# The first batch of an attention and mixing kernel run group by group, with joint folds and a second bank for the first products

## The chip, the cores and the metric

The kernel runs on one core of a Trainium2 chip. The metric is device time in microseconds (us), the median of several executions. One further execution was taken by the hardware profiler; its rows are times within that one execution, counted from the start of its span. Engines are named PE (TensorE, matrix products), DVE (VectorE), ACT (ScalarE), POOL (GpSimd) and SP (the engine that issues most loads and stores).

## The reference

The inputs are q, k, v of shape (8, 8, 576, 64) (batch, heads, positions, head size), 32 packed queries p for each head, and two weights of 512x2048 and 2048x512.

```python
def sm_attn(qq, kk, vv):
    s = scale * np.matmul(qq, kk.transpose(0, 1, 3, 2))
    s = s - np.max(s, axis=-1, keepdims=True)
    a = np.exp(s)
    a = a / (np.sum(a, axis=-1, keepdims=True) + 1e-09)
    return np.matmul(a, vv)
p_packed = sm_attn(p, k, v)
out = sm_attn(q, p_packed, p_packed)
# x = out with the heads side by side: (8, 576, 512)
X = np.fft.fft(x, axis=1)
X = np.fft.fft(X, axis=2)
u = x + np.real(X)
mu = np.mean(u, axis=-1, keepdims=True)
var = np.mean((u - mu) ** 2, axis=-1, keepdims=True)
un = (u - mu) / np.sqrt(var + 1e-06)
ch = np.maximum(un @ w_ch1, 0.0) @ w_ch2
return u + ch
```

## The kernel before

Each batch has a front (attention and the two Fourier transforms, which give rows of u) and then shares of nine tiles of 512 rows through the two weight products. The fronts of batches 1 to 7 run in between the products of the tile before; the front of batch 0 has nothing ahead of it. Products of 32-bit values are made from a high and a low part (`split`: ScalarE rounds to the high part, another engine takes the rest), three products for one.

**The front** works on two groups g of four heads. Its steps have one letter each, and a written list `ORDER` (one string for batch 0, one for the others) sets their order; as scheduling is manual for PE, DVE, ACT and POOL, each engine executes its instructions as this order issues them. In batch 0: K, V, Q, B, W load keys, values, queries, tables and weight blocks on SP; S makes the scores of the packed queries and their exponentials for both groups (`scores`, tiles s1 and s1t in the code, s and s1t in the profile), t turns them, p and c make the packed values (pp) and a block diagonal of them (bd, and its parts bdh, bdl), d and l turn and split those (ppT, pph, ppl); U makes the scores of the queries (s2T) for both groups, u turns them on VectorE (`turned_queries`), e subtracts the maximum and exponentiates (`less_one`), m subtracts the mean (`less_mean`), w and b scale and turn to a (`scaled`, `upright`). G makes products of the packed values with a Fourier basis (pg), T turns their phases (`values_turned`), z splits the result into gh and gl. f folds a by its symmetries into eo and f (`folded`), r makes the small rest of f (`folded_rest`, on GpSimd in batch 0), h splits f into fh and fl, x splits eo (xh, xl, oh, ol). P multiplies fh, fl with gh, gl for all six parts of the spectrum (`waves_of`, the waves py) and splits each into yh and yl behind the second group. H unpacks a weight block on ScalarE (`halves_of`), `joined` ends that on VectorE, and L issues the loads of four tables on GpSimd and one on SP.

After the waves, `value` multiplies the parts of eo with the block diagonal (px) and `spectrum` the splits with the tables (pz, copied to spec); from both VectorE makes pe, qe and then two blocks of 128 rows of u, twice. `Turned` subtracts the mean (un), turns a block on PE (untp) and splits it (uh, ul).

**The products.** `up(j)` multiplies uh, ul with weight block j of w1 into a bank ph, ScalarE and VectorE make hh and hl of it, and `down(j)` multiplies these with block j of w2 into four accumulators. The weight blocks' parts wr_h (ScalarE) and wr_l (GpSimd) come from a generator, `splits`. The first `up` runs in two halves of 256 rows in one bank.

**PSUM** has eight banks: four accumulators, one for ph, and a ring of three (tag `ps`). `bank` takes the next one of the ring or, while the accumulators are spare (in batch 0's front), one of these. A tile that is taken from the ring waits for the last reader of the tile three before it.

The order behind the front's list is in the code that calls it, with `next(gen0)` for each stretch of batch 0's generator up to its next yield:

```python
        next(gen0)
        for k in (0, 2):
            joined(k // 2, k % 2)
        next(splits)
        next(splits)
        ...
        centred(3)
        cur.parts(2)
        cur.parts(3)
        for k in (1, 3, 4, 5):
            joined(k // 2, k % 2)
```

## Time and profile before

| | us |
|---|---|
| Median of 3 executions | 989.1 (988.87 to 991.14) |
| Profiled execution, whole | 990.03 |
| Profiled execution, span of its instructions | 988.3 |
| PE busy | 952.2 (96% of the span) |
| VectorE busy | 555.2 (56%) |
| ScalarE busy | 474.4 (48%) |
| GpSimd busy | 469.1 (47%) |
| First product of up(0) | 54.49 |
| First product of up(1) | 64.63 |

A row of a timeline has the start in us, the length, the engine, the line of the kernel, the operation, the tile written and those read, partitions and columns, and a count if several were merged; in brackets stands how long the engine was idle before it and what ended that. The chain of waits is followed back from the last instruction to what released each. A PE row's length holds the time through the array, so that rows overlap; the distance from start to start is what a product costs in a stream. PE's rows of 32-bit operands come twice, as two passes.

### The profile page before, as it was taken

Reading aid. Unit: us, or ns where it says so; the run is one execution under the profiler, and the core shown is the slowest. Engines: PE = TensorE matmul, PEld = TensorE weight load, DVE = VectorE, ACT = ScalarE, POOL = GpSimd, SP = SyncE. Lnnn points to the kernel's source line nnn. Section 1 sums busy time; section 2 is a strip of 40 time slices with the busy share of each in tenths; the row PEclk is TensorE's granted clock in tenths of the full one; section 3 lists DMA queues with packets and bytes.
Section 4 is the critical chain, followed back from the end, with each engine's and each line's share of the span. In section 5 each row is a group of like instructions: output and inputs, shape, how many; then the busy total and the mean of one; then the engine's idle time right before and its main releaser. Section 6 shows DMA issues by size and latency. Waiting matters only on the chain.

```text
span 988.3 us, 15063 instructions
## 1 busy us (share of the span) xinstructions
PE 952.2 (96%) x5588; PEld 783.8 (79%) x5588; DVE 555.2 (56%) x1224; ACT 474.4 (48%) x956; POOL 469.1 (47%) x409
## 2 busy tenths in 40 slices
...
GB/s 363 114 75 203 161 180 65 127 26 1 20 136 63 1 2 141 49 1 22 100 118 0 9 60 162 9 1 55 136 49 1 22 65 1 1 31 55 1 1 43
DMA packets 28170, 65.94 MB, mean 67 GB/s; under 512 B 5494, under 2 KB 12992, under 8 KB 28096
## 3 DMA queue, kind: packets, MB, share of 16 engines
...
q8 instruction: 44, 0.72, 0.3%
q14 instruction: 30, 0.25, 0.1%
...
## 4 chain that ended last, share of the span: by engine, by line
PE 90%; DVE 4%; ACT 3%; DMA 1%; issue 1%; POOL 0%; SPq 0%; DVEq 0%; ACTq 0%; POOLq 0%
PE ph L780 38%; PE acc L795 38%; PE po L323 1%; PE py L236 1%; PE py L234 1%; PE py L235 1%; PE px L234 1%; PE px L236 1%; PE px L235 1%; PE e1tp L300 1%; PE s L266 1%; PE s2T L266 1%; PE pz L234 1%; PE pz L236 1%; PE pz L235 1%
## 5 line engine op out<-in xcount | busy, mean ns | idle before, releaser
L100 POOL TENSOR_TENSOR wr_l<-w1f,wr_h 128x512 fp32r<-128x512 f32 x144 | 194.6, 1352 | 280.1 <-ACT wr_h L99 237.9
L785 DVE SCALAR_TENSOR_TENSOR hl<-ph,hh 128x512 fp32r<-128x512 f32 x144 | 98.9, 687 | 335.6 <-ACT hh L784 335.2
L100 POOL TENSOR_TENSOR wr_l<-w2f,wr_h 128x512 fp32r<-128x512 f32 x144 | 192.3, 1336 | 173.1 <-ACT wr_h L99 166.3
L780 PE MATMUL ph<-uh,wr_h 128*128 128x512 f32 (+1 forms) x580 | 228.7, 395 | 3.8 <-DVE hl L785 2.3
L795 PE MATMUL acc<-wr_h,hh 128*128 128x512 f32 x576 | 226.2, 393 | 0.0
L780 PE MATMUL ph<-uh,wr_l 128*128 128x512 f32 (+1 forms) x580 | 225.4, 389 | 0.0
L795 PE MATMUL acc<-wr_h,hl 128*128 128x512 f32 x576 | 225.2, 391 | 0.0
L795 PE MATMUL acc<-wr_l,hh 128*128 128x512 f32 x576 | 225.2, 391 | 0.0
L780 PE MATMUL ph<-ul,wr_h 128*128 128x512 f32 (+1 forms) x580 | 220.8, 389 | 0.0
L784 ACT ACTIVATE hh<-ph 128x512 fp32r<-128x512 f32 x144 | 86.2, 599 | 206.4 <-PE ph L780 192.3
L780 PEld LDWEIGHTS ph<-uh,wr_h 128*128 128x128 f32 x580 | 108.9, 188 | 38.8 <-DVE mx L285 5.9
L780 PEld LDWEIGHTS ph<-uh,wr_l 128*128 128x128 f32 x580 | 108.9, 188 | 23.1
L795 PEld LDWEIGHTS acc<-wr_h,hl 128*128 128x128 f32 x576 | 108.2, 188 | 23.2
L780 PEld LDWEIGHTS ph<-ul,wr_h 128*128 128x128 f32 x580 | 109.0, 189 | 20.7
L795 PEld LDWEIGHTS acc<-wr_h,hh 128*128 128x128 f32 x576 | 108.2, 188 | 21.8
L795 PEld LDWEIGHTS acc<-wr_l,hh 128*128 128x128 f32 x576 | 108.2, 188 | 21.3
L99 ACT CAST wr_h<-w1f 128x512 fp32r<-128x512 f32 x144 | 88.9, 618 | 55.9 <-POOL wr_l L100 54.2
L99 ACT CAST wr_h<-w2f 128x512 fp32r<-128x512 f32 x144 | 88.3, 613 | 12.4 <-PE acc L795 8.1
L234 PE MATMUL py<-gh,fh 128*128 128x258 f32 (+2 forms) x96 | 29.1, 303 | 14.4 <-ACT fh L529 14.4
L213 ACT ACTIVATE junk<-ubuf,stat 128x512 f32<-128x512 f32 x36 | 25.6, 713 | 25.0 <-DVE stat L209 25.0
L100 POOL TENSOR_TENSOR gl<-turned,gh 128x516 fp32r<-128x516 f32 x16 | 24.6, 1535 | 26.3 <-ACT gh L99 26.3
L236 PE MATMUL py<-gh,fl 128*128 128x258 f32 (+2 forms) x96 | 29.0, 302 | 2.6 <-DVE fl L531 2.6
...
## 6 DMA issues: line engine op xcount, KB each, us to landing
...
w1f<-w SPq DMA_DIRECT2D x3, 512.0 KB, 10.4
```

What stands on the lines that cost most here:

```text
L99: nc.scalar.copy(hi, src)
L100: (lo_eng or nc.vector).tensor_tensor(lo, src, hi.bitcast(F32), ALU.subtract)
L213: nc.scalar.activation(junk, u, AF.Square, bias=st[:, 1:2], scale=1.0, accum_out=st[:, 2:3])
L234: nc.tensor.matmul(o, lh, rh, start=first, stop=False)
L235: nc.tensor.matmul(o, lh, rl, start=False, stop=False)
L236: nc.tensor.matmul(o, ll, rh, start=False, stop=last)
L266: nc.tensor.matmul(res[g][c][at, :w.stop - w.start], lhs(g, h), rhs(g, h, w), start=True, stop=True, tile_position=(r, h * NPK))
L300: nc.tensor.transpose(tp[g][:, c * P:(c + 1) * P], e1s[g][:, c * P:(c + 1) * P], ident)
L780: nc.tensor.matmul(ph[:, t], l[:, c * P:(c + 1) * P], r[:, c, t], start=(n == 0), stop=(n == 11))
L784: nc.scalar.activation(hh[:, :T], ph[:, :T], AF.Relu)
L785: nc.vector.scalar_tensor_tensor(hl[:, :T], ph[:, :T], 0.0, hh[:, :T].bitcast(F32), ALU.max, ALU.subtract)
L795: nc.tensor.matmul(acc[i], l[:, w], r, start=(j == 0 and k == 0), stop=(j == NJ - 1 and k == 2))
```

## The change

- **By group.** In batch 0 the scores S and the queries U are issued for one group at a time (s0, s1, q0, q1), and the turn of the queries (v0, v1) stands in each group's own part of the list. The list's other steps move too: ScalarE's weight blocks H, the loads L (now behind gl and s of group 1 on GpSimd), and the splits z of gh and gl.
- **Joint folds.** In `folded` two instructions make what four made: both halves of a pair in one access pattern with a step between them (`pair`). `folded_rest` does the same with its small parts. This holds for all batches.
- **Parts of f.** In batch 0 fh and fl are made in two pieces, columns 0 to 421 and 421 to 776.
- **Waves.** Their order changes, the last of them takes the bank ph, and the first two px are made between the waves of group 0 and those of group 1 (X). The join and the split of the first weight block come behind the fourth wave.
- **First products.** The first `up` takes two banks, ph and one of the ring, for its two halves; it makes the products with the high parts of both halves first, then those with the low parts. Blocks 2 and 3 of u are turned in banks of the ring, between the two halves. The low parts of u, five joins and the split of two weight blocks come behind that.

VectorE, from the last rows of u to the first hl. Before, two of the ul (low parts of u) stood ahead of these rows (L640), and four joins (L174) behind the other two:

```order
L100 TENSOR_TENSOR ul<-untp,uh 128x4x4x32 [waits Activation_49] x2
L640 SCALAR_TENSOR_TENSOR ubuf,stat<-qe,pe 128x512 [waits DVE_49]
L209 TENSOR_SCALAR stat<-stat 128x1 [waits DVE_49]
L640 SCALAR_TENSOR_TENSOR ubuf,stat<-qe,pe 128x512
L209 TENSOR_SCALAR stat<-stat 128x1 [waits DVE_49]
L100 TENSOR_TENSOR ul<-untp,uh 128x4x4x32 [waits Activation_49] x2
L174 SCALAR_TENSOR_TENSOR w2f<-w2f 128x512 [waits DMAHW2_49]
L174 SCALAR_TENSOR_TENSOR w2f<-w2f 128x512 [waits DMAHW4_49]
L174 SCALAR_TENSOR_TENSOR w1f<-w1f 128x512 [waits DMAHW5_49]
L174 SCALAR_TENSOR_TENSOR w2f<-w2f 128x512 [waits DMAHW6_49]
L785 SCALAR_TENSOR_TENSOR hl<-ph,hh 128x512 [waits Activation_49]
```

The same place after:

```order
L651 SCALAR_TENSOR_TENSOR ubuf,stat<-qe,pe 128x512 [waits DVE_49]
L209 TENSOR_SCALAR stat<-stat 128x1 [waits DVE_49]
L651 SCALAR_TENSOR_TENSOR ubuf,stat<-qe,pe 128x512
L209 TENSOR_SCALAR stat<-stat 128x1 [waits DVE_49]
L766 TENSOR_TENSOR ul<-untp,uh 128x4x4x32 [waits Activation_49] x4
L174 SCALAR_TENSOR_TENSOR w1f<-w1f 128x512 [waits DMAHW3_49]
L174 SCALAR_TENSOR_TENSOR w2f<-w2f 128x512
L174 SCALAR_TENSOR_TENSOR w2f<-w2f 128x512 [waits DMAHW4_49]
L174 SCALAR_TENSOR_TENSOR w1f<-w1f 128x512 [waits DMAHW7_49,DMAHW5_49]
L174 SCALAR_TENSOR_TENSOR w2f<-w2f 128x512 [waits DMAHW6_49]
L812 SCALAR_TENSOR_TENSOR hl<-ph,hh 128x256 [waits Activation_49] x2
```

All four ul stand behind the rows of u now, a fifth join (w1's second block, L174) ahead of hl, and hl comes in two.

PE, at the px (rows of eo's parts with the block diagonal). Before, they followed the last wave of group 1:

```order
L234 MATMUL py<-gh,fh 128x258
L235 MATMUL py<-gl,fh 128x258
L236 MATMUL py<-gh,fl 128x258
L234 MATMUL px<-bdh,xh 128x256 [waits PE_49]
L235 MATMUL px<-bdl,xh 128x256
L236 MATMUL px<-bdh,xl 128x256
```

After, twelve products px stand behind the last wave of group 0, and the first wave of group 1 behind them:

```order
L234 MATMUL px<-bdh,oh 128x256 [waits Activation_49]
L235 MATMUL px<-bdl,oh 128x256
L236 MATMUL px<-bdh,ol 128x256 [waits DVE_49]
L234 MATMUL py<-gh,fh 128x258 [waits Activation_49]
L235 MATMUL py<-gl,fh 128x258 [waits Pool_49]
L236 MATMUL py<-gh,fl 128x258 [waits DVE_49]
```

So the spectra pz follow the last wave of group 1 directly.

PE, at the scores of batch 1 (acc and s by their banks), which stand between the last spectra of batch 0 and up(1). Before:

```order
L266 MATMUL acc_626<-kp 32x64
L266 MATMUL acc_627<-kp 32x64
L266 MATMUL acc_626<-kp 32x64
L266 MATMUL acc_627<-kp 32x64
L266 MATMUL s_700<-kp 32x512
L266 MATMUL s_701<-kp 32x512 [waits Activation_49]
```

After:

```order
L266 MATMUL acc_599<-kp 32x64
L266 MATMUL acc_600<-kp 32x64
L266 MATMUL acc_599<-kp 32x64
L266 MATMUL acc_600<-kp 32x64
L266 MATMUL s_697<-kp 32x512 [waits DVE_49]
L266 MATMUL s_698<-kp 32x512 [waits Activation_49]
```

Group 0's scores wait for VectorE now: their bank of the ring is that of the second half of the first `up`, whose last reader is the second hl. The same instructions of PE are issued in both kernels, 5012 of them; behind up(0) their order is the same.

The diff, cut to its core:

```diff
-ORDER = ("K0 K1 I0 V0 V1 Q0 Q1 B0 W0 W1 W2 W3 S t0 t1 p0 p1 d0 d1 l0 l1 U N c0 W4 W5 c1 L0 W6 W7 W8 H0 H1 e0 u G0 e1 "
-         "H2 T0 z0 G1 m0 w0 b0 H3 H4 f0 r0 m1 w1 T1 h0 z1 P0 H5 b1 f1 r1 x0 h1 x1 P1",
+ORDER = ("K0 K1 I0 V0 V1 Q0 Q1 B0 W0 W1 W2 W3 s0 s1 t0 t1 p0 p1 d0 d1 l0 l1 q0 q1 N c0 W4 W5 c1 W6 W7 W8 H0 v0 e0 "
+         "G0 T0 z0 v1 G1 H1 e1 L0 H2 m0 w0 b0 f0 r0 m1 H3 w1 T1 h0 P0 H4 H5 b1 z1 f1 x0 r1 x1 X0 h1 P1",
          "S y X y p0 c0 p1 c1 y d0 l0 d1 l1 y g0 y U y g1 y e0 y e1 y y m0 y a0 y m1 y a1 y f0 y r0 y h0 x0 y f1 y r1 y h1 x1 y y")
...
             s2Ts.update(s2T)
-            if b == 0:
-                turned_queries(1, *gs)
-                turned_queries(0, gs[0])
-                return
-            for c in (1, 0):
-                turned_queries(c, *reversed(gs))
-
-        def turned_queries(c, *gs):
-            w = (slice(0, 16), slice(16, 18))[c]
-            for g in gs:
-                nc.vector.transpose(s2s[g][:, w, :].rearrange("p a k -> p (a k)"), s2Ts[g][c])
+            if b > 0:
+                turned_queries(*reversed(gs))
+
+        def turned_queries(*gs):
+            for c, w in ((1, slice(16, 18)), (0, slice(0, 16))):
+                for g in gs:
+                    nc.vector.transpose(s2s[g][:, w, :].rearrange("p a k -> p (a k)"), s2Ts[g][c])
         def less_one(g):
...
             as_[g] = a
+
+        def pair(f, at, to, *inner):
+            w = f[:, at:at + 1]
+            return bass.AP(tensor=w.tensor, offset=w.offset, ap=[list(w.ap[0]), [to - at, 2], *[list(x) for x in inner]])
         def folded(g):
...
             e2.tensor_tensor(oc[:, 0:287], a[:, 0:287], a[:, NE:S], ALU.subtract)
-            e3.tensor_tensor(f[:, 0:128], ec[:, 0:128], ec[:, 144:272], ALU.add)
-            e3.tensor_tensor(f[:, 128:256], ec[:, 0:128], ec[:, 144:272], ALU.subtract)
-            e4.tensor_tensor(f[:, FO:FO + 128], oc[:, 0:128], oc[:, 144:272], ALU.subtract)
-            e4.tensor_tensor(f[:, FO + 128:FO + 256], oc[:, 0:128], oc[:, 144:272], ALU.add)
+            x, y = eo[:, :, 0:128], eo[:, :, 144:272]
+            e3.tensor_tensor(pair(f, 0, FO + 128, [1, 128]), x, y, ALU.add)
+            e4.tensor_tensor(pair(f, 128, FO, [1, 128]), x, y, ALU.subtract)
             eos[g], fs[g] = eo, f
         def constants(f, eng):
...
+            def three_times(x):
+                return x.unsqueeze(2).to_broadcast([P, 2, 3, x.shape[-1]])
+
+            def ends(at, op):
+                sm.tensor_tensor(fe3[:, :, at:at + 1], a[:, 287:288].unsqueeze(1).to_broadcast([P, 3, 1]),
+                                 a[:, 288:289].unsqueeze(1).to_broadcast([P, 3, 1]), op)
+
+            if b == 0:
+                ends(16, ALU.add)
+                ends(32, ALU.subtract)
+            x, y = three_times(eo[:, :, 128:143]), three_times(eo[:, :, 272:287])
+            sm.tensor_tensor(pair(f, FR, FOR + 15, [33, 3], [1, 15]), x, y, ALU.add)
+            sm.tensor_tensor(pair(f, FR + 17, FOR, [33, 3], [1, 15]), x, y, ALU.subtract)
+            if b > 0:
+                ends(16, ALU.add)
+                ends(32, ALU.subtract)
+            middle = (pair(f, FR + 15, FOR + 30, [33, 3], [1, 1]), three_times(eo[:, :, 143:144]))
             doubled = ((f[:, FA:FA + 33], a[:, 256:289]), (f[:, FA + 33:FA + 64], a[:, NE + 256:S]))
             if b > 0:
-                for o, x in middles:
-                    sm.tensor_copy(o, x.unsqueeze(1).to_broadcast([P, 3, 1]))
+                sm.tensor_copy(*middle)
                 constants(f, sm)
                 for o, x in doubled:
                     sm.tensor_scalar(o, x, 2.0, 1.0 / 16, ALU.mult, ALU.add)
             else:
                 for o, x in doubled:
                     nc.scalar.activation(o, x, AF.Copy, scale=2.0, bias=1.0 / 16)
-                for o, x in middles:
-                    nc.scalar.copy(o, x.unsqueeze(1).to_broadcast([P, 3, 1]))
+                nc.scalar.copy(*middle)
             xh[g] = work.tile([P, 256], F32R, tag="xh", name="xh")
             nc.scalar.activation(xh[g], ec[:, 0:256], AF.Copy, bias=1.0 / 16)
             oh[g] = work.tile([P, 256], F32R, tag="oh", name="oh")
...
             eo, f = eos[g], fs[g]
             ec, oc = eo[:, 0, :], eo[:, 1, :]
             fh[g] = work.tile([P, FW], F32R, tag="fh", name="fh")
-            nc.scalar.copy(fh[g], f)
             fl[g] = work.tile([P, FW], F32R, tag="fl", name="fl")
-            nc.vector.tensor_tensor(fl[g], f, fh[g].bitcast(F32), ALU.subtract)
+            for w in ([slice(0, FO), slice(FO, FW)] if b == 0 else [slice(0, FW)]):
+                split(fh[g][:, w], fl[g][:, w], f[:, w])
         def values_rest(g):
...
-        WAVES = [(0, 0), (1, 0), (0, None), (1, None), (0, 1), (1, 1)]
+        WAVES = [(0, 0), (0, None), (1, 0), (1, None), (0, 1), (1, 1)]
         yh, yl, yr = {}, {}, {}
         def wave(t, c, gs):
...
         def waves_of(g):
             for at in WAVES:
                 if g == 0:
-                    pys[at] = bank("py")
+                    pys[at] = psf.tile([P, 512], F32, tag="ph", name="py") if at == (1, 1) else bank("py")
                 wave(*at, (g,))
                 if g == 1:
                     wave_split(*at)
-
-        parts = {"S": lambda _: scores(0, 1), "U": lambda _: queries(0, 1), "X": lambda _: turned_scores(0, 1),
+                    if at == (1, None):
+                        joined(0, 0)
+            if g == 1:
+                next(splits)
+
...
+
+        early = []
+
+        def first_values():
+            early.extend(value(h, l, slice(1, 256, 2)) for h, l in ((xh, xl), (oh, ol)))
+
+        parts = {"S": lambda _: scores(0, 1), "s": scores, "q": queries, "U": lambda _: queries(0, 1), 
...
             for c in range(2):
-                px = [side_value(n, c) for n in range(2)]
+                px = early if c == 0 else [side_value(n, c) for n in range(2)]
                 AB = spectrum(0, c), spectrum(1, c)
...
             else:
                 nc.vector.tensor_scalar(self.un[i], u_of[key], stat_of[key][:, 1:2], None, ALU.add)
-        def moves(self, i):
-            un, tp = self.un[i], bank("untp")
+        def moves(self, i, own=False):
+            un, tp = self.un[i], ps.tile([P, 512], F32, tag="ps", name="untp") if own else bank("untp")
             self.tp[i] = tp.rearrange("p (c q k) -> p q c k", c=4, q=4)
             def move(c):
...
             pool, tag = (ps, "ps") if alone and j % 2 else (psf, "ph")
-            ph = pool.tile([P, 512], F32, tag=tag, name="ph")
-
-            step = T // 2 if first == 0 and j < SPL else T
+            ph = [pool.tile([P, 512], F32, tag=tag, name="ph")]
+            tokens, runs = [slice(0, T)], [range(12)]
+            if first == 0 and j < SPL:
+                ph.append(ps.tile([P, 512], F32, tag="ps", name="ph"))
+                tokens, runs = [slice(0, T // 2), slice(T // 2, T)], [range(8), range(8, 12)]
             order = sorted(range(12), key=lambda k: k % 3 == 1) if j == 0 else range(12)
-            for t in (slice(i, i + step) for i in range(0, T, step)):
-                for n, k in enumerate(order):
-                    c, (l, r) = k // 3, ((wh, uh), (wh, ul), (wl, uh))[k % 3]
-                    nc.tensor.matmul(ph[:, t], l[:, c * P:(c + 1) * P], r[:, c, t], start=(n == 0), stop=(n == 11))
+            for run in runs:
+                for o, t in zip(ph, tokens):
+                    for n in run:
+                        c, (l, r) = order[n] // 3, ((wh, uh), (wh, ul), (wl, uh))[order[n] % 3]
+                        nc.tensor.matmul(o[:, t], l[:, c * P:(c + 1) * P], r[:, c, t], start=(n == 0), stop=(n == 11))
+                    while turned.meanwhile:
+                        turned.meanwhile.pop(0)()
             next(splits, None)
             hh = work.tile([P, 512], F32R, tag="hh", name="hh")
             hl = work.tile([P, 512], F32R, tag="hl", name="hl")
-            nc.scalar.activation(hh[:, :T], ph[:, :T], AF.Relu)
-            nc.vector.scalar_tensor_tensor(hl[:, :T], ph[:, :T], 0.0, hh[:, :T].bitcast(F32), ALU.max, ALU.subtract)
+            for o, t in zip(ph, tokens):
+                nc.scalar.activation(hh[:, t], o[:, t], AF.Relu)
+                nc.vector.scalar_tensor_tensor(hl[:, t], o[:, t], 0.0, hh[:, t].bitcast(F32), ALU.max, ALU.subtract)
             return hh, hl
         def down(j, hh, hl, moves=()):
...
         next(gen0)
-        for k in (0, 2):
-            joined(k // 2, k % 2)
-        next(splits)
-        next(splits)
         next(gen0)
         next(gen0)
         centred(0)
         next(gen0)
         centred(1)
         next(gen0)
-        cur.parts(0)
-        cur.parts(1)
+        cur.high(0)
+        cur.high(1)
         next(gen0)
-        centred(2)
+        cur.less(2, True)
         next(gen0)
-        centred(3)
-        cur.parts(2)
-        cur.parts(3)
-        for k in (1, 3, 4, 5):
-            joined(k // 2, k % 2)
+        cur.less(3, True)
+        cur.low(0)
+        cur.low(1)
+        cur.meanwhile = cur.moves(2, True) + cur.moves(3, True)
+
+        def others():
+            for i in (2, 3):
+                cur.high(i)
+            for i in (2, 3):
+                cur.low(i)
+            joined(1, 0)
+            next(splits)
+            for k in (1, 3, 4, 5):
+                joined(k // 2, k % 2)
+
+        cur.meanwhile.append(others)
         assert next(gen0) == "rest"
     spare.clear()
     rest = gen0
```

62 lines of the change are left out of this document (29 added, 33 removed).

## Prediction

> **What bounds the kernel now.** I read the windows by stage first, then PE's waits, then the chain of waits through the first 90 us, and last the timelines of the engines that the chain names there.
>
> ```profile
> 21.30:45.10 23.80, 9.20 (x37) 8.31 (x38) 21.59 (x44) 15.06 (x34) 12.56 (x27) 0.50 0.50 176
> ...
> 55.50:58.80 3.30, 3.15 (x14) 2.37 (x13) 1.39 (x7) 2.03 (x3) 0.00 (x0) 0.50 0.00 0
> ...
> 160.00:900.00 740.00, 740.00 (x4348) 612.27 (x4347) 426.14 (x951) 340.33 (x693) 358.85 (x296) 1.00 0.16 50
> ```
> ```profile
> PE ph L780 <- DVE hl L785: 2.3, 3, 1.0
> ```
>
> The windows' columns are length, then busy time and instructions of PE, weight loads, VectorE, ScalarE, GpSimd, then PE's granted clock. From 160 on PE is busy 740.00 of 740.00 us, and after 64 it waits three times for hl, 2.3 us together. So work that only makes VectorE, ScalarE or GpSimd lighter there is worth nothing; what counts is when PE's unbroken stream begins. Before it PE is busy 9.20 us of the 23.80 between 21.30 and 45.10 while VectorE is busy 21.59: the first batch's front is VectorE's. I therefore take one clock for the whole case: the start of the products of the second weight block (up(1)), behind which PE hardly waits.
>
> ```profile
> 4.82 0.42 PE L266 MATMUL s1t<-kp 64*32 64x64 f32 x2 [4.82 <-DMA kp<-kpT]
> 6.38 0.36 PE L266 MATMUL s1t<-kp 64*32 64x64 f32 x7 [1.14 <-DMA kp<-kpT]
> ...
> 36.05 0.58 PE L236 MATMUL py<-gh,fl 128*128 128x258 f32 x1 [2.39 <-DVE fl L531]
> ...
> 41.31 0.58 PE L236 MATMUL py<-gh,fl 128*128 128x258 f32 x1 [0.20 <-DVE fl L531]
> ...
> 46.48 0.28 PE L234 MATMUL pz<-yh,tbh 128*128 128x258 f32 x1
> ...
> 56.83 1.97 PE L720 MATMUL untp<-ident,un 128*128 128x128 f32 x8 [0.15 <-ACT un L711]
> ...
> 62.91 1.79 PE L266 MATMUL s<-kp 64*32 64x512 f32 x16
> 64.63 0.50 PE L780 MATMUL ph<-uh,wr_h 128*128 128x512 f32 x1
> ```
> ```profile
> 16.89 0.95 PE s2T L266 x15
> ...
> 37.55 1.85 POOL f L498 x6
> ...
> 39.42 0.84 ACT fh L529
> ...
> 40.29 0.98 DVE fl L531
> ...
> 41.89 0.22 PE py L234
> ...
> 45.32 0.12 PE px L235
> ```
>
> The first fence is PE's timeline (start, length, what, and in brackets its idle time and who ended it), the second the chain. PE waits 2.39 us for group 0's fl, then for group 1's, starts the spectra (pz) at 46.48 and up(1) at 64.63. Products of some 256 columns follow each other by 0.22 us at 41.89 and by 0.12 at 45.32: that is the step from the granted clock of 0.50 to the full one.
>
> **The change, part by part.** Durations are those of the profiled execution, 990.03 us (span 988.3 and 1.7 around it), 0.9 above the median of 989.1.
>
> ```profile
> 17.83 0.72 DVE L390 STREAM_TRANSPOSE s<-s2T 128x512 f32<-128x512 f32 x1 [0.35 <-PE s2T L266]
> ...
> 28.87 1.37 DVE L478 TENSOR_TENSOR f<-eo 128x128 f32<-128x128 f32 x1
> ...
> 30.78 0.37 DVE L481 TENSOR_TENSOR f<-eo 128x128 f32<-128x128 f32 x1
> 31.07 0.74 DVE L409 TENSOR_REDUCE z<-s 128x18 f32<-128x576 f32 x1
> ...
> 33.71 1.40 DVE L436 TENSOR_TENSOR turned<-turned 128x258 f32<-128x258 f32 x2
> ...
> 35.91 0.77 DVE L460 STREAM_TRANSPOSE a<-s 128x576 f32<-128x576 f32 x1
> 36.71 0.75 DVE L476 TENSOR_TENSOR eo<-a 128x287 f32<-128x287 f32 x1
> ...
> 41.17 0.42 DVE L538 SCALAR_TENSOR_TENSOR xl<-eo,xh 128x256 fp32r<-128x256 f32 x1
> ...
> 48.96 1.51 DVE L640 SCALAR_TENSOR_TENSOR ubuf<-qe,pe 128x512 f32<-128x512 f32 x1
> ...
> 50.58 1.57 DVE L640 SCALAR_TENSOR_TENSOR ubuf<-qe,pe 128x512 f32<-128x512 f32 x1
> ...
> 53.61 0.69 DVE L100 TENSOR_TENSOR ul<-untp,uh 128x512 fp32r<-128x512 f32 x1
> ...
> 55.87 0.68 DVE L640 SCALAR_TENSOR_TENSOR ubuf<-qe,pe 128x512 f32<-128x512 f32 x1
> ...
> 60.06 1.28 DVE L174 SCALAR_TENSOR_TENSOR w2f<-w2f 128x512 int32<-128x512 int32 x2
> ...
> 61.86 1.80 DVE L174 SCALAR_TENSOR_TENSOR w2f<-w2f 128x512 int32<-128x512 int32 x1
> 63.58 0.68 DVE L785 SCALAR_TENSOR_TENSOR hl<-ph,hh 128x512 fp32r<-128x512 f32 x1
> ```
> ```profile
> 28.59 1.50 POOL L100 TENSOR_TENSOR gl<-turned,gh 128x516 fp32r<-128x516 f32 x1 [3.27 <-ACT gh L99]
> ...
> 35.84 1.31 POOL L100 TENSOR_TENSOR gl<-turned,gh 128x516 fp32r<-128x516 f32 x1 [1.35 <-ACT gh L99]
> ...
> 48.62 2.98 POOL L100 TENSOR_TENSOR wr_l<-w1f,wr_h 128x512 fp32r<-128x512 f32 x2 [9.24 <-ACT wr_h L99]
> 61.47 1.64 POOL L100 TENSOR_TENSOR wr_l<-w2f,wr_h 128x512 fp32r<-128x512 f32 x1 [9.87 <-ACT wr_h L99]
> ```
> ```profile
> 56.05 1.52 ACT L711 ACTIVATE un<-ubuf,stat 128x512 f32<-128x512 f32 x2 [1.61 <-DVE stat L209]
> ...
> 58.83 0.59 ACT L99 CAST uh<-untp 128x512 fp32r<-128x512 f32 x1 [0.27 <-PE untp L720]
> 60.77 0.62 ACT L99 CAST wr_h<-w2f 128x512 fp32r<-128x512 f32 x1 [1.35 <-DVE w2f L174]
> ```
>
> *A, scores and queries by group, to the turn of s2T (17.83).* PE stood 1.14 us, to 6.38, for group 1's keys. Alone, group 0 starts at 4.82, 1.56 earlier. But the sixteen passes of both groups run side by side (fifteen of s2T in 0.95), so one group takes as long as two, and group 1's scores now come a full length later. Between nothing (group 1 sets the time, since its pp2 stands in PE's order ahead of group 0's s2T) and -1.5; I take the middle, -0.8, because s2T of group 0 no longer waits behind group 1's ppT, and the rest of the softmax is still one queue on ScalarE.
>
> *B, the folds of group 0.* Four rows from 28.87 to 31.07, 2.20 us. The first took 1.37 where its like takes 0.37, and it ended when GpSimd's gl (28.59, 1.50 long) ended: VectorE and GpSimd exclude each other when both take two SBUF inputs. Now two rows of 256 columns; the nearest such row is 0.42 (41.17), about 0.37 apart, so 0.75. gl now stands ahead of GpSimd's table loads and is done by then. -1.45; if GpSimd is still in the way, -0.4.
>
> *C, from there to a of group 1 (31.07 to 35.91).* The same rows. The collision at 33.71 (1.40 for two, with GpSimd's product of s and z) stays, and fl in two parts costs one start, 0.1. Zero, between -0.6 (collision gone) and +0.6 (one more).
>
> *D, from a of group 1 to the first pz (35.91 to 46.48, 10.57).* Let A be the start of the transpose. It takes 0.77, the two eo 0.8. gh and gl of group 1 are now issued behind two more weight blocks on ScalarE, so gl no longer lies beside the transpose but beside eo or the folds, where it costs up to 1.2 as at 28.87: A+2.8. Two folds, 0.75. GpSimd's small parts, 1.85 for six in the chain, are four, 1.4, and end at A+5.0. The first part of fh and of fl is 421 of 776 columns, 0.5 each (of 0.84 and 0.98): A+6.1. Eighteen products at 0.215, 3.9, and 0.4 for starts: A+10.4, so -0.2. What is won is the px: twelve products that stood between the last wave and pz now run ahead of group 1's waves. Bounds: with the clock as it was and no collision -1.4; with PE's stream unbroken (group 0's waves, px, group 1's waves) the full clock can come before 45.2, worth another 1.2, since then the splits of the waves on VectorE set the time (-2.6); with a further collision +0.7.
>
> *E, from pz to the last rows of u (46.48 to 56.55).* The two u rows at 48.96 and 50.58 took 1.51 and 1.57 against 0.68 (55.87): GpSimd made two wr_l, 2.98, there. Only one block is now joined ahead of this, so only one wr_l, which starts with ScalarE's wr_h directly behind the waves and falls beside pe and qe, which read PSUM. That removes 0.83 and 0.89. The two ul (0.69 at 53.61, its fellow behind it), 1.5 with the wait between them, move behind the u rows. Together -3.2; if one u row still meets the wr_l, and pz runs at half clock, -1.5.
>
> The Trainium skill (SBUF — State Buffer, "Who interferes with whom") has VectorE contend with a GpSimd instruction that reads SBUF only when VectorE takes two SBUF inputs or runs in a two-port mode. By it pe and qe, with one input in PSUM, lose nothing beside the wr_l; the trace shows no such pair, and if both lost 0.4, E would be -2.4 and the sum -2.9.
>
> *F, from the last u row to up(1).* Before: 56.55 to 64.63, 8.1. Call the end of u U. Now un, turn, uh and ul of block 3 follow: 0.76+0.66+0.59+0.69, with 0.25 of starts U+2.95 (half the un row of 56.05; 0.66 is four of the eight turns of 56.83 at full clock, a third of 1.97). Then, on VectorE, five joins ahead of hl instead of four: 0.6 each, 3.0. Two wr_l come free during them (w1's second block and w2's first) instead of one. In the row at 61.86 one wr_l (61.47, 1.64) made a join 1.80 instead of 0.68: +1.12, twice 2.24. Then hl in two parts, 0.85: U+9.05. Here the change adds a wait: hl's second part reads the second bank, which is taken from the three banks of the ring; the third tile taken after it, batch 1's first scores, needs that bank, so on PE scores and all of up(1) queue behind it. The scores take 1.1 to 1.8 (0.95 in the chain, 1.79 at 62.91): U+10.2, +2.1. PE itself has less: second half, low parts and pz at 0.12, done about U+5.8. If no wr_l meets a join, hl ends at U+6.8 and up(1) starts at U+7.9, -0.2; at worst, with the slow scores and the half clock, +3.2.
>
> *The rest.* The four tables go to their queue later on GpSimd, whose next work is a's parts; they are wanted at pz, some 15 us after their issue: zero. The DMA of sels passes three weight loads on SP, wanted 18 us later: zero. Joint folds of batches 1 to 7 take some ten rows off VectorE in each, under a PE that does not wait: zero, but for the 2.3 us of waits for hl in the first tile, of which VectorE's folds are a part; I put -0.15, between 0 and -0.5.
>
> Sum: -0.8 -1.45 +0 -0.2 -3.2 +2.1 -0.15 = -3.7. On the profiled execution 986.3, on the median **985.4 us** (989.1 - 3.7).
>
> **The rivals.** *No hold at hl.* The joins run while GpSimd is idle or have passed before wr_h is ready; F is then -0.2 and the sum -6.0: 983.1. For it: wr_h at 60.77 began 0.7 behind the start of its join (60.06), so the first two or three joins are free. Against it: wr_l follows within 0.1 of wr_h (61.47), and the joins that remain are back to back.
>
> *Full clock inside D.* Group 0's waves, px and group 1's waves make one stream of 48 products, 10.3 us at 0.215. If the clock rises in its first two thirds, group 1's eighteen take 2.2 instead of 3.9; VectorE's splits, 0.4 to 0.5 for each of six waves, hold some of that up. D -1.5 instead of -0.2: sum -5.0, 984.1. For it: the full stretch behind 41.31 ended in the full clock. Against it: the 3.9 us behind 36.05 did not.
>
> The Trainium skill (TensorE: Matmul & The Clock Gate, "What's actually happening") says that the full clock follows a busy window of about 3.4 us of a free-running grid. By that rule 10.3 us always hold a busy window, and the sum is -5.0; the 3.9 us that did not raise the clock agree with it only if they lay across two windows, which no row here shows.
>
> *Mostly given back.* Another collision in C or D, A at nothing, and the hold in full: A 0, C +0.6, F +2.6, the rest as above, -1.6 or so: 987.5. For it: collisions of 0.3 to 1.1 show at 28.87, 33.71, 36.71, 48.96, 50.58 and 61.86, and the change only moves GpSimd's work. This includes that a part does not do what it says: gl that leaves the transpose meets the folds.
>
> *Slower: PE at half clock through the transition.* The clock was 0.50 in the window to 45.1 although eighteen products ran behind each other from 36.05 (3.9 us), rose with a stretch that was full from 41.31, and was 0.50 again from 55.5. If the new pauses at pz and un keep it at 0.50 until up(1) is done, then by the rows 0.22 and 0.12: eight products of pz on the path 0.8; twenty px and pz beside pe and u take 4.4 instead of 2.4 and so hold the second pe by 1.3; the turn of block 3, 0.98 instead of 0.66, 0.3; the scores at 1.8, 0.8; twelve products of 512 columns in up(1) at 0.44 instead of 0.23, 2.5. The low parts and last spectra hide behind the hold at hl. Together 5.7, 2.0 later than now: 991.1. It passes the time of before when the lost clock costs more than 3.7, which the first four alone (3.2) do not. For it: PE has 1 to 2 us pauses in this stretch now; against it: px joins the waves of both groups to one stream.
>
> **How the numbers follow.** Changes within 0.3% (3.0 us) of 989.1 are about what a measurement of this kernel cannot tell from none: 986.1 to 992.1. Forecast, 984.5 to 986.1: 0.34. Full clock inside D, 984.1: 0.13. No hold, 983.1: 0.15. Given back, about 987.5: 0.28. Half clock, around 991.1: 0.10, half of it on either side of 992.1, since A's or C's worst would come on top. So faster 0.62, same 0.33, slower 0.05. The range leaves out that last case and the far half of the bounds: its low end is the sum with no hold and D's full clock together (-7.3, 981.8), its high end the case of what is given back with 1.3 more for a slow pz and slow scores (988.8).
>
> **What would show it.** In the profile of after: the first scores at 4.8 and s2T's turn near 17.0; two f rows of about 0.42 in place of four; px between the waves of the two groups; one wr_l ahead of the u rows, and u rows of 0.68; five join rows behind the last ul, of which two are near 1.8; PE idle 1 to 3 us ahead of batch 1's scores, ended by hl; up(1) at 60.5 to 61.5. The prediction is wrong if the idle time stands elsewhere, if up(1) starts later than 63, or if PE, once it has begun, waits more than 2.5 us in the first tile.

## The result and the profile after

| | before | after |
|---|---|---|
| Median, us | 989.0 (988.87 to 991.14, 4 executions) | 999.32 (998.14 to 999.52, 4 executions) |
| Profiled execution, whole | 990.03 | 999.18 |
| Its span | 988.3 | 997.4 |
| First product of up(1) | 64.63 | 59.90 |
| From there to the end of the span | 923.7 | 937.5 |

The change makes the kernel slower: the ratio is 1.0097, with a 95% interval of 1.0079 to 1.0114. The front gained more than was forecast: up(1) starts 4.73 us earlier, against 3.55. The rest of the kernel, in which the prediction looked for 0.15 us, became 13.8 us longer. PE does the same products there in the same order.

The windows of the profile after, over the stretch in which PE never waits, and over the last stretch in which there is no front beside the products (columns as in the prediction):

```profile
160.00:900.00 740.00, 740.00 (x4298) 603.27 (x4298) 418.49 (x876) 334.19 (x682) 349.40 (x292) 1.00 0.15 49
860.00:960.00 100.00, 100.00 (x433) 81.14 (x432) 21.02 (x30) 35.56 (x63) 46.65 (x36) 1.00 0.07 22
```

The last of these of the kernel before:

```profile
860.00:960.00 100.00, 100.00 (x442) 82.79 (x442) 21.68 (x31) 36.29 (x64) 48.61 (x37) 1.00 0.07 22
```

PE is busy all the time at the full granted clock in both, yet it did 433 products in these 100 us and had done 442. The timelines of PE near 900 us show what one product takes. Before, twelve steps from one start to the next lie between these two rows:

```profile
899.95 0.39 PE L780 MATMUL ph<-uh,wr_h 128*128 128x512 f32 x1
...
902.67 0.39 PE L795 MATMUL acc<-wr_h,hh 128*128 128x512 f32 x1
```

After, twelve steps lie between these:

```profile
900.06 0.40 PE L822 MATMUL acc<-wr_l,hh 128*128 128x512 f32 x1
...
902.86 0.40 PE L822 MATMUL acc<-wr_l,hh 128*128 128x512 f32 x1
```

A product of 512 columns follows the one ahead of it by 2.72/12 = 0.2267 us before and by 2.80/12 = 0.2333 after (in `down`; a table below has 229.9 ns for `up`). Over all 3443 products of `up` and `down` from up(1) on (512 columns each), the distances from start to start add up to 794.9 us before and 808.9 after: these 14.0 us are the loss. The products of 256 columns and less keep their distances.

The waits of PE, after, from 54 us to the end, answer to the one row that was shown of before:

```profile
PE ph L804 <- DVE hl L812: 2.6, 3, 1.4
PE s L266 <- DVE stat L216: 2.5, 1, 2.5
```

The wait for hl in the first tile is as before (2.6 after 2.3); the new one is the predicted hold at batch 1's scores (the row names stat, which stands directly behind the second hl on VectorE; the bank is hl's). PE's timeline after, at the places that the prediction speaks of:

```profile
4.71 0.44 PE L266 MATMUL s1t<-kp 64*32 64x64 f32 x8 [4.71 <-DMA kp<-kpT]
...
31.23 0.58 PE L234 MATMUL py<-gh,fh 128*128 128x258 f32 x1 [13.59 <-ACT fh L99]
...
33.17 0.58 PE L236 MATMUL py<-gh,fl 128*128 128x258 f32 x1 [1.15 <-DVE fl L100]
...
38.85 0.28 PE L234 MATMUL px<-bdh,oh 128*128 128x256 f32 x1
38.97 0.28 PE L235 MATMUL px<-bdl,oh 128*128 128x256 f32 x1
...
42.10 0.28 PE L234 MATMUL pz<-yh,tbh 128*128 128x258 f32 x1
...
47.14 1.45 PE L731 MATMUL untp<-ident,un 128*128 128x128 f32 x8 [1.50 <-ACT un L722]
...
58.88 1.09 PE L266 MATMUL s<-kp 64*32 64x512 f32 x16 [2.46 <-DVE stat L216]
59.90 0.50 PE L804 MATMUL ph<-uh,wr_h 128*128 128x512 f32 x1
```

VectorE's:

```profile
16.12 0.72 DVE L386 STREAM_TRANSPOSE s<-s2T 128x512 f32<-128x512 f32 x1
...
27.52 0.43 DVE L479 TENSOR_TENSOR f<-eo 128x256 f32<-128x256 f32 x1
27.98 0.43 DVE L480 TENSOR_TENSOR f<-eo 128x256 f32<-128x256 f32 x1
28.32 0.75 DVE L405 TENSOR_REDUCE z<-s 128x18 f32<-128x576 f32 x1
...
33.48 0.77 DVE L456 STREAM_TRANSPOSE a<-s 128x576 f32<-128x576 f32 x1
...
36.33 0.43 DVE L479 TENSOR_TENSOR f<-eo 128x256 f32<-128x256 f32 x1 [1.22 <-POOL f L484]
...
44.05 0.69 DVE L642 TENSOR_TENSOR pe<-px,spec 128x512 f32<-128x512 f32 x1 [0.30 <-ACT spec L592]
...
45.44 0.69 DVE L651 SCALAR_TENSOR_TENSOR ubuf<-qe,pe 128x512 f32<-128x512 f32 x1
...
47.04 0.68 DVE L642 TENSOR_TENSOR pe<-px,spec 128x512 f32<-128x512 f32 x1
...
49.22 0.68 DVE L651 SCALAR_TENSOR_TENSOR ubuf<-qe,pe 128x512 f32<-128x512 f32 x1
...
54.70 1.78 DVE L174 SCALAR_TENSOR_TENSOR w1f<-w1f 128x512 int32<-128x512 int32 x1
56.41 1.75 DVE L174 SCALAR_TENSOR_TENSOR w2f<-w2f 128x512 int32<-128x512 int32 x1
58.08 0.75 DVE L812 SCALAR_TENSOR_TENSOR hl<-ph,hh 128x256 fp32r<-128x256 f32 x2
```

And GpSimd's:

```profile
34.71 1.54 POOL L100 TENSOR_TENSOR gl<-turned,gh 128x516 fp32r<-128x516 f32 x1 [2.72 <-ACT gh L99]
...
43.82 1.29 POOL L100 TENSOR_TENSOR wr_l<-w1f,wr_h 128x512 fp32r<-128x512 f32 x1 [5.01 <-ACT wr_h L99]
54.31 1.62 POOL L100 TENSOR_TENSOR wr_l<-w1f,wr_h 128x512 fp32r<-128x512 f32 x1 [9.20 <-ACT wr_h L99]
55.90 1.71 POOL L100 TENSOR_TENSOR wr_l<-w2f,wr_h 128x512 fp32r<-128x512 f32 x1
```

The scores start at 4.71, the turn of s2T stands at 16.12, the folds are two rows of 0.43, px run in the full clock from 38.85 (the next follows in 0.12), pz starts at 42.10, all four rows of u take 0.68 or 0.69, two joins take 1.78 and 1.75 beside the two wr_l, and PE stands 2.46 us to 58.88.

### The profile page after: what moved, and what is told of

Its sections match the earlier page's. It is cut to its first block, busy times and chain, and to the rows that moved or that the text cites. A ratio compares the mean times of both kernels' runs of the same rounds, so it can differ in the third digit from the quotient of the medians.

```text
span 997.4 us, 14993 instructions
## 1 busy us (share of the span) xinstructions
PE 963.9 (97%) x5588; PEld 781.5 (78%) x5588; DVE 552.7 (55%) x1153; ACT 473.9 (48%) x957; POOL 462.9 (46%) x405
## 4 chain that ended last, share of the span: by engine, by line
PE 90%; DVE 4%; ACT 3%; DMA 1%; issue 1%; POOL 1%; DVEq 0%; ACTq 0%; POOLq 0%
PE acc L822 38%; PE ph L804 38%; PE po L323 1%; PE py L236 1%; PE py L234 1%; PE py L235 1%; PE s L266 1%; PE px L236 1%; PE px L234 1%; PE px L235 1%; PE e1tp L300 1%; PE pz L234 1%; PE pz L236 1%; PE pz L235 1%; PE s2T L266 1%
## 5 line engine op out<-in xcount | busy, mean ns | idle before, releaser
L100 POOL TENSOR_TENSOR wr_l<-w1f,wr_h 128x512 fp32r<-128x512 f32 x144 | 192.6, 1337 | 294.2 <-ACT wr_h L99 254.8
L812 DVE SCALAR_TENSOR_TENSOR hl<-ph,hh 128x512 fp32r<-128x512 f32 (+1 forms) x145 | 99.6, 687 | 346.0 <-ACT hh L811 345.8
L100 POOL TENSOR_TENSOR wr_l<-w2f,wr_h 128x512 fp32r<-128x512 f32 x144 | 188.6, 1309 | 172.8 <-ACT wr_h L99 172.2
L822 PE MATMUL acc<-wr_h,hh 128*128 128x512 f32 x576 | 228.7, 397 | 0.0
L822 PE MATMUL acc<-wr_l,hh 128*128 128x512 f32 x576 | 228.2, 396 | 0.0
L822 PE MATMUL acc<-wr_h,hl 128*128 128x512 f32 x576 | 228.0, 396 | 0.0
L804 PE MATMUL ph<-uh,wr_l 128*128 128x512 f32 (+1 forms) x580 | 227.3, 392 | 0.0
L811 ACT ACTIVATE hh<-ph 128x512 fp32r<-128x512 f32 (+1 forms) x145 | 86.4, 596 | 215.7 <-PE ph L804 214.9
L217 POOL TENSOR_TENSOR stat<-stat,mhalf 128x1 f32<-128x1 f32 x36 | 24.3, 690 | 11.5 <-DVE stat L216 11.5
```

The costliest lines, as they stand in the source:

```text
L100: (lo_eng or nc.vector).tensor_tensor(lo, src, hi.bitcast(F32), ALU.subtract)
L217: nc.gpsimd.tensor_tensor(st[:, 2:3], st[:, 2:3], mhalf, ALU.pow)
L804: nc.tensor.matmul(o[:, t], l[:, c * P:(c + 1) * P], r[:, c, t], start=(n == 0), stop=(n == 11))
L811: nc.scalar.activation(hh[:, t], o[:, t], AF.Relu)
L812: nc.vector.scalar_tensor_tensor(hl[:, t], o[:, t], 0.0, hh[:, t].bitcast(F32), ALU.max, ALU.subtract)
L822: nc.tensor.matmul(acc[i], l[:, w], r, start=(j == 0 and k == 0), stop=(j == NJ - 1 and k == 2))
```

## What could make every product slower

In that stretch no product, no order of PE and no granted clock differs between the two kernels, and VectorE only has some rows fewer. What differs is where the weight parts lie in SBUF. A pool places the buffers of a tag when its first tile is asked for. The change asks for the first wr (with `next(splits)` at the end of `waves_of`) ahead of the first `spec`; before, it was the other way round. So six buffers wr that began at byte 194432 of a partition begin at 192320 now, and the two spec lie behind them. Every other working buffer lies where it lay. A product has a stationary operand, which a weight load brings into PE ahead of it, and a moving one, which then runs through column by column. In `up` wr is the stationary operand and uh or ul the moving one; in `down` hh or hl is stationary and wr moves. Modulo 256, wr began at 128, like uh, ul, hh and hl, and begins at 64 now.

Theories: the place of wr ("place", later "phase": its first byte modulo 256 against that of the other operand); the ring of PSUM banks, which stands otherwise ("banks"); a stream that runs slower because the work ahead of it is denser ("load").

## The experiments

### The place of wr, moved back and moved over

`e1_spec_first`, the changed kernel with one thing moved; no instruction differs:

```diff
+        specs = []
+
         def waves_of(g):
...
             if g == 1:
+                specs.extend(work.tile([P, N2], F32, tag=f"spec{t}", name=f"spec{t}", bufs=1) for t in range(2))
                 next(splits)
...
-            sb = work.tile([P, N2], F32, tag=f"spec{t}", name=f"spec{t}", bufs=1)
+            sb = specs.pop(0) if specs else work.tile([P, N2], F32, tag=f"spec{t}", name=f"spec{t}", bufs=1)
```

> The changed kernel, with the two tiles spec allocated ahead of the weight buffers wr, so that all buffers lie in SBUF where they lay before the change (wr at byte 194432 of a partition, a multiple of 128; in the changed kernel it is 192320, a multiple of 64 only). No instruction and no order changes. Theory 'place': the 512-column products lose 227 to 233 ns each because of wr's place; they go back to 227 ns from start to start, up(1) starts near 59.9 as in the changed kernel, and the time is that of before less the 4.7 us by which up(1) starts earlier (64.63 to 59.90): 984.3, between 983.5 and 985.0. Rival 'banks' (the change takes another number of PSUM banks ahead of the stream, so the ring stands otherwise against ph): 999.3 as the changed kernel. Rival 'load' (the stream itself runs slower once the front is denser): 999.3.

Measured: 984.52 us (983.88 to 991.03), ratio to the kernel before 0.9959 (0.9947 to 0.9972). The window of e1's profile:

```profile
860.00:960.00 100.00, 100.00 (x443) 82.81 (x442) 21.01 (x30) 36.27 (x63) 48.31 (x38) 1.00 0.07 22
```

443 products in 100 us, up(1) at 58.74, and from there to the last product 919.1 us (919.4 before, 932.8 after the change). "Place" holds; "banks" and "load" would have left 999.3.

`e2_before_wr_first` does the opposite to the kernel before:

```diff
+                    if at == (1, 1):
+                        pre.extend(work.tile([P, DM], F32R, tag="wr", name=n, bufs=6) for n in ("wr_h", "wr_l"))
...
-                hi = work.tile([P, DM], F32R, tag="wr", name="wr_h", bufs=6)
+                hi = pre.pop(0) if pre else work.tile([P, DM], F32R, tag="wr", name="wr_h", bufs=6)
...
```

> The kernel before, with the weight buffers wr allocated ahead of spec, so that wr lies at 192320 as in the changed kernel and everything else where it was. No instruction and no order changes. Theory 'place': products of 512 columns at 231 to 233 ns in the stream instead of 227, up(1) at 64.6 as before, time 989.0 + 13.8 (the time from up(1) to the end was 923.7 before and 937.5 after the change) = 1002.8, between 1001.5 and 1004. Rivals 'banks' and 'load': 989.0, nothing changes.

Measured: 1002.67 (1001.95 to 1003.44), ratio 1.0138 (1.0123 to 1.0153). Its window:

```profile
860.00:960.00 100.00, 100.00 (x433) 81.11 (x432) 21.02 (x30) 35.59 (x62) 46.59 (x36) 1.00 0.07 22
```

The same 433 products as after the change, and the time to within 0.2 of what was worked out. The place alone, without any of the change, costs 13.1 us against the median of the kernel before beside it (989.52).

### Which property of the place

`e3_wr_ahead_of_yr` is the changed kernel with the same `pre.extend` ahead of the first yr; `e4_one_spec_first` is e1 with `range(1)` for `range(2)`.

> The changed kernel, with wr allocated ahead of yr and spec: wr at 190208, another place than in either kernel, but a multiple of 128. If what counts is whether the buffers begin at a multiple of 128 bytes: 984.3 and steps of 227 ns. If it is another property of the place (its distance from other buffers, the region that it lies in, or the tiles behind it): between 984 and 1003, near 999.3 if it is what lies below 194432.

> The changed kernel, with one of the two tiles spec allocated ahead of wr: wr at 193376, which is 96 over a multiple of 128. If any place off a multiple of 128 costs the same: 999.3. If it is the part of a row of 2048 or 512 bytes that lies across a 64-byte line: more than 999.3, 1003 to 1015, since at 96 (32 over a multiple of 64) every piece of 64 bytes is cut as well. If only 64 bytes over hurts: 984.3.

Measured: e3 1000.84 (999.80 to 1001.26), ratio 1.0115 (1.0102 to 1.0128); e4 1001.37 (1000.91 to 1005.98), 1.0132 (1.0116 to 1.0148). Their windows, e3's first:

```profile
860.00:960.00 100.00, 100.00 (x433) 81.08 (x432) 21.02 (x30) 35.66 (x62) 46.30 (x37) 1.00 0.07 22
```

```profile
860.00:960.00 100.00, 100.00 (x431) 80.41 (x430) 21.01 (x30) 35.64 (x62) 46.09 (x36) 1.00 0.07 22
```

So a multiple of 128 is not what counts: 190208 is one, and costs as much. Two of e4's cases fall too, that only 64 bytes over hurts (984.3) and that cut pieces of 64 bytes cost more (1003 to 1015). The numbers 190208, 192320 and 193376 lie 0, 64 and 96 over a multiple of 256, and the good 194432 lies 128 over, as do uh, ul, hh and hl. That made the next theory, with three kernels to test it.

```diff
 # f1_wr_at_192384, on the changed kernel: wr stays ahead of spec
-            yr[t] = work.tile([P, N2], F32R, tag=f"yr{t}", name="yr", bufs=1)
+            yr[t] = work.tile([P, N2 + 16 * t], F32R, tag=f"yr{t}", name="yr", bufs=1)[:, :N2]
-            sb = work.tile([P, N2], F32, tag=f"spec{t}", name=f"spec{t}", bufs=1)
+            sb = work.tile([P, N2 + 48 * t], F32, tag=f"spec{t}", name=f"spec{t}", bufs=1)[:, :N2]
 # f2_all_64_on, on e1
-    sels = cpool.tile([P, 1], F32, name="sels")
+    sels = cpool.tile([P, 17], F32, name="sels")[:, :1]
 # f3_hh_64_on, on e1: ul is 64 bytes longer, hh and hl lie behind it
+                self.hl = [work.tile([P, 4 * 512 + 16 * m], F32R, tag=n, name=n, bufs=1)[:, :4 * 512].rearrange("p (c t) -> p c t", c=4)
+                           for m, n in enumerate(("uh", "ul"))]
```

> The changed kernel with wr still ahead of spec, and two tiles made longer: yr by 64 bytes, so that wr begins at 192384, and spec by 192, so that un, ul, hh and hl move by 256 in all. So wr lies within 64 bytes of its place in the changed kernel, but at 128 over a multiple of 256, as uh, ul, hh and hl do (wr was at 128 over in the kernel before, and at 64, 0 and 96 over in the three slow ones). Theory 'phase': a product is fast if its two operands begin at the same byte modulo 256; steps 227 ns, 984.5 (983.5 to 985.5). Rival 'absolute': a product is fast if its operands begin at 128 over 256; 984.5 too. Rival 'neighbours' (what hurts is which tiles lie behind wr, or the place as such): 999 to 1001.

> The kernel with spec first, and a tile of one column (sels) that lies ahead of all working buffers made 64 bytes longer: uh, ul, hh, hl and wr all move by 64 and begin at 192 over a multiple of 256. Only the tables, the identity and the weights stay. Theory 'phase' (the two operands against each other): 227 ns and 984.5. Rival 'absolute' (each at 128 over 256, or at a multiple of 128): products at 231 to 234 ns, 999 to 1002. Rival 'neighbours': 984.5.

> The kernel with spec first, and ul made 64 bytes longer, so that hh and hl alone move by 64; wr, uh and ul stay where they were. Theory 'phase': the products of down (stationary hh or hl, moving wr) go to about 233 ns, those of up (stationary wr, moving uh or ul) stay at 227 but for the first few behind each down; half of the loss, 984.5 + 7 to 10 = 991 to 995. Rival 'absolute': the same here. Rival 'wr alone counts': 984.5.

Measured: f1 985.70 (984.25 to 989.96), ratio 0.9971 (0.9956 to 0.9985); f2 984.36 (983.64 to 985.28), 0.9952 (0.9938 to 0.9965); f3 995.69 (995.19 to 999.74), 1.0075 (1.0057 to 1.0092). f1 lies 64 bytes beside the place that cost 13.8 us, with spec behind wr, and loses nothing in its stream, which takes 919.0 us from up(1) to the last product: "neighbours" falls. (Its median lies 0.2 over the expected range; up(1) starts at 60.24 in its profile, where e1 has 58.74.) f2 has every working buffer at 192 over 256 and loses nothing: "absolute" falls. In f3 wr lies well and hh and hl do not; it loses 11, a little more than the 7 to 10 expected.

Two more kernels ask for the other pair and the other sign: in `h1_uh_ul_64_on` gl and un are made 64 bytes longer (in two buffers of 32 each) and uh and ul 192, so that only uh and ul stand off; in `h2_wr_64_over` the second spec is made 64 longer and un 192, so that wr stands 64 over the others.

> The kernel with spec first, with uh and ul alone moved to 64 over the byte of wr, hh and hl modulo 256 (gl and un are made longer ahead of them, uh and ul behind them). If products lose whenever stationary and moving operand differ modulo 256: up's products (moving uh, ul) at 231 to 234 ns, the first ones of each down slower too, 984.5 + 8 to 11 = 992 to 996, as with hh and hl moved (995.7). If only down's products lose, and what up showed in the slow kernels (228.9 and 229.9 ns) was the transition behind them: 984.5 to 986.

> The kernel with spec first, with wr alone moved to 64 over the byte of uh, ul, hh and hl modulo 256 (it was 64 under it in the changed kernel, at 999.3). If the offset counts by its size: 999 (997 to 1002). If its sign decides which operand waits for which: down or up at 227 ns, 986 to 994.

Measured: h1 992.88 (991.62 to 995.47), ratio 1.0039 (1.0025 to 1.0053); h2 999.68 (999.09 to 999.81), 1.0100 (1.0085 to 1.0115). All nine together; the steps are means from start to start over the products between 135 and 35 us ahead of the last one:

| kernel | wr | uh, ul | hh, hl (first byte modulo 256) | step in up, ns | step in down, ns | us |
|---|---|---|---|---|---|---|
| before | 128 | 128 | 128 | 226.7 | 226.7 | 989.0 |
| after | 64 | 128 | 128 | 229.9 | 233.4 | 999.3 |
| e1 | 128 | 128 | 128 | 226.7 | 226.7 | 984.5 |
| e2 (order of before) | 64 | 128 | 128 | 229.9 | 233.4 | 1002.7 |
| e3 | 0 | 128 | 128 | 232.0 | 232.0 | 1000.8 |
| e4 | 96 | 128 | 128 | 233.0 | 233.6 | 1001.4 |
| f1 (wr and spec as after) | 128 | 128 | 128 | 226.7 | 226.7 | 985.7 |
| f2 | 192 | 192 | 192 | 227.3 | 227.1 | 984.4 |
| f3 | 128 | 128 | 192 | 228.9 | 233.2 | 995.7 |
| h1 | 128 | 192 | 128 | 230.2 | 230.6 | 992.9 |
| h2 | 192 | 128 | 128 | 233.3 | 231.6 | 999.7 |

Where all of them agree modulo 256, a step is 227 ns, wherever they lie; where a pair differs, by 32 or 128, or by 64 in either direction, it is 3 to 7 ns more. That 256 itself costs nothing shows in the kernel before: wr and uh begin at 194432 and 161408, an odd multiple of 256 apart. In f3 and h1 the products whose own operands agree lose some too (228.9 and 230.6), but not all of them. By their place in each run of twelve, the first six steps of f3's `up` take 228 to 236 ns and the others 227; in h1's `down` the steps are at 227 from the eleventh on. So the disturbance outlasts the products that cause it and then dies out. What in the memory or in PE's reads has this period of 256 bytes no run here shows. Nor does one show whether a product's own two operands count or its moving one and the next product's stationary one, which is loaded beside it; nor other offsets than these, nor operands of other types or lengths.

### The front

With the place mended, four things in the front could be tried; each of these kernels has wr, uh, ul, hh and hl at 128.

`g3_both_groups`, on e1, undoes the order by group:

```diff
-ORDER = ("... W3 s0 s1 t0 t1 p0 p1 d0 d1 l0 l1 q0 q1 N ...
+ORDER = ("... W3 S t0 t1 p0 p1 d0 d1 l0 l1 U N ...
```

> The kernel with spec first, and the scores and queries of batch 0 issued for both groups at once again (S for s0 s1, U for q0 q1); the turns of s2T stay in two. In the two profiles VectorE's first turn of s2T stood at 17.83 before and at 16.12 after the change, 1.71 earlier, where the prediction put 0.8. If the order by group is worth that: first scores pass at 6.4 instead of 4.7, the turn near 17.8, time 984.5 + 1.7 = 986.2 (985.5 to 987.0). By the prediction's term 985.3. If the keys simply came earlier in that run: 984.5.

Measured: 987.77 (986.25 to 988.61), ratio 0.9979 (0.9969 to 0.9988). That is 3.2 us over e1's median, but 2.0 us by the two ratios, whose intervals overlap a little; so it is likely that the order by group helps, and its size is open. The turn of s2T stands at 17.91 in it. With the order by group it stood at 16.12 in the profile of the changed kernel and at 15.01 in e1's, which has the same instructions. PE's rows show the difference; the turns of the exponentials in the kernel before:

```profile
10.79 1.11 PE L300 MATMUL e1tp<-ident,e 128*128 128x128 f32 x4 [2.25 <-ACT e L291]
...
11.91 1.06 PE L300 MATMUL e1tp<-ident,e 128*128 128x128 f32 x4
```

in the changed kernel:

```profile
9.09 1.12 PE L300 MATMUL e1tp<-ident,e 128*128 128x128 f32 x4 [0.68 <-ACT e L291]
...
10.64 1.11 PE L300 MATMUL e1tp<-ident,e 128*128 128x128 f32 x4 [0.22 <-ACT e L291]
```

and in e1:

```profile
9.09 0.66 PE L300 MATMUL e1tp<-ident,e 128*128 128x128 f32 x4 [0.71 <-ACT e L291]
...
10.61 0.66 PE L300 MATMUL e1tp<-ident,e 128*128 128x128 f32 x4 [0.74 <-ACT e L291]
```

The same four products take 1.12 us in one execution and 0.66 in the other. By their lengths PE runs at about half speed in the one until 13 us and is at full speed from 9 in the other, though the clock column says 1.00 for both. In the profile of g3 these rows take 1.12 and 1.06. So the order by group brings the first scores 1.7 us forward (6.38 to 4.71), and in some executions the full clock comes early enough for the turns as well. The rows are at 0.66 in seven of the thirteen profiles of kernels with this order and in none of the three of the other; three are too few to show that the order brings the full clock.

`f4_hl_ahead`, on e1, takes away the hold at hl: the last two joins stand behind hl.

```diff
-            for k in (1, 3, 4, 5):
+            for k in (1, 3):
                 joined(k // 2, k % 2)
+            cur.last = [lambda k=k: joined(k // 2, k % 2) for k in (4, 5)]
...
                 nc.vector.scalar_tensor_tensor(hl[:, t], o[:, t], 0.0, hh[:, t].bitcast(F32), ALU.max, ALU.subtract)
+            while turned.last:
+                turned.last.pop(0)()
```

> The kernel with spec first, and the two hl of the first products issued on VectorE ahead of the last two joins (L174) instead of behind them. In the changed kernel PE stands 2.46 us at batch 1's scores, to 58.88, for the second hl (58.08, 0.75 for both), which stands behind two joins of 1.78 and 1.75 that ran beside wr_l. If that hold is what sets up(1): hl ends near 55.9, the scores follow the small ones at 56.1 to 56.4, up(1) starts at 57.4 instead of 59.9: 984.5 - 2.5 = 982.0 (981.4 to 982.8). If the later joins only move the wait (batch 1's maxima come later, then its exponentials, for which PE waits, or the weight parts of up(2)): 983.5 to 985.

Measured: 984.08 (982.12 to 987.10), ratio 0.9946 (0.9932 to 0.9959); that lies in the rival's range, and beside e1's 0.9959 it is unclear. In its profiled execution, the one of 987.1, the hold is gone, but PE ran at a clock of 0.61 from 46 to 57 us (up(1) starts at 61.47), and stood 1.49 ahead of the turns of u. First the window, then PE's timeline:

```profile
46.00:57.00 11.00, 8.03 (x35) 6.99 (x36) 8.64 (x22) 6.54 (x11) 0.48 (x1) 0.61 0.00 0
```

```profile
47.48 1.91 PE L734 MATMUL untp<-ident,un 128*128 128x128 f32 x8 [1.49 <-ACT un L725]
```

`g2_filled` puts seventeen products that nobody reads into these pauses:

```diff
+    def turning(n):
+        d = psf.tile([P, 512], F32, tag="ph", name="d")
+        for _ in range(n):
+            nc.tensor.matmul(d[:, :N2], basis[:, 0, 0:P], basis[:, 1, :], start=True, stop=True)
+
     def centred(i):
         cur.less(i, True)
+        turning((10, 3)[i])
...
         cur.high(1)
+        turning(4)
```

> The kernel with spec first and hl ahead of the last two joins, and seventeen products that nobody reads put into PE's pauses ahead of the first turns (untp) and the first products: ten, three and four of 258 columns. In the profile of the kernel without them PE stood 1.49 us ahead of the turns at 47.48 and its granted clock was 0.50 from there to 57, at 987.1 us; its five times ran from 982.1 to 987.1. Theory 'clock': PE keeps the full clock there, times from 981.8 to 983.5, median 982.4. Rival: the pause is not what lowers the clock, the spread stays (982 to 987) and the median is 984.1, or 0.3 more for products that stand ahead of the turns.

Measured: 982.96 (982.16 to 984.31), ratio 0.9936 (0.9924 to 0.9949). Its window, and its rows of PE:

```profile
46.00:57.00 11.00, 10.06 (x94) 7.63 (x93) 10.22 (x23) 8.99 (x19) 3.37 (x3) 1.00 0.01 1
```

```profile
44.10 1.36 PE L890 MATMUL d<-basis 128*128 128x258 f32 x10
45.77 0.66 PE L734 MATMUL untp<-ident,un 128*128 128x128 f32 x4 [0.30 <-ACT un L725]
...
54.86 1.97 PE L266 MATMUL s<-kp 64*32 64x512 f32 x16
56.76 0.50 PE L807 MATMUL ph<-uh,wr_h 128*128 128x512 f32 x1
```

The clock stays at 1.00 in that execution, the highest of five times falls from 987.10 to 984.31, and the median is 0.6 over what was expected. The intervals of f4 and g2 overlap, and the profile of e1 has the same pause (1.50) with a clock of 1.00, so that the pause does not always lower the clock; that the filling helps is likely but not shown. What the hold costs can be read from the rows: from the start of the last row of u to up(1) it was 10.68 after the change (49.22 to 59.90) and is 8.91 here (47.85 to 56.76). So 1.8 were to be had, not 2.5: the large scores take 1.97 when they follow the small ones directly and 1.09 when they had waited.

`g1_gl_earlier`, on f4, issues group 1's split z1 between H4 and H5 and sets both groups' constants of f at once; `g4_earlier_and_filled` has this and the filling.

> The kernel with spec first and hl ahead of the last two joins, and group 1's split z1 issued between the weight steps H4 and H5 instead of behind H5 and b1; the constants of both groups' f are set with group 0's. In the changed kernel VectorE stood 1.22 us ahead of group 1's first fold (36.33) for GpSimd, whose gl (34.71, 1.54) waited for ScalarE's two weight steps. If that wait is on the path: gh at 32.9, gl 33.5 to 35.0, the first eo ends with it, folds at 35.8 instead of 36.33: 984.1 - 0.5 = 983.6 (983.0 to 984.2). If the fold is hidden behind ScalarE's fh or the collision moves to the eo in full: 984.1 or 0.3 more.

> Both edits, the earlier gl and the seventeen products in PE's pauses, on the kernel with spec first and hl ahead of the last two joins. If both act: 982.4 - 0.5 = 981.9 (981.2 to 983.0). If neither: 984.1.

Measured: g1 984.60 (982.65 to 985.75), ratio 0.9947 (0.9933 to 0.9962); g4 982.49 (981.62 to 985.35), 0.9926 (0.9913 to 0.9940). In the profile of g1 the fold waits no more: VectorE's rows

```profile
33.37 0.77 DVE L456 STREAM_TRANSPOSE a<-s 128x576 f32<-128x576 f32 x1
34.17 0.78 DVE L477 TENSOR_TENSOR eo<-a 128x287 f32<-128x287 f32 x1
...
35.35 0.43 DVE L480 TENSOR_TENSOR f<-eo 128x256 f32<-128x256 f32 x1
```

show 1.98 from the transpose to the first fold, where it was 2.85 (33.48 to 36.33); the collision with gl has moved to the first eo (0.78 for 0.46). The times of g1 do not tell it from f4 (983.6 was expected). g4 is the best version here, 0.7% under the kernel before, and its interval lies below that of e1.

## Why the prediction was wrong

The forecast was 985.4, faster; the kernel takes 999.3 and is slower. The step that failed is the first one, in "what bounds the kernel now": "I therefore take one clock for the whole case: the start of the products of the second weight block (up(1)), behind which PE hardly waits." PE waits no more than before behind it, that was right. But "PE is busy" was taken to mean that its products take what they took. The change moved wr in SBUF, and each product of 512 columns became 4 ns longer on average, 3443 times. No rival had that: all of them lie ahead of up(1), and the one that ended slower, half clock in the transition, had another mechanism; the granted clock was 1.00 there. The sign that was named for a wrong prediction ("if PE, once it has begun, waits more than 2.5 us in the first tile") stands at 2.6 after 2.3 and has no part in it: the loss is no wait. With wr put back (e1) the kernel takes 984.5, within 0.9 of the forecast; part of that is luck, since A, D and E below miss by 0.9, 1.75 and 0.9, the last of them the other way. The rival "mostly given back" is -1.8 by its own terms, not -1.6; nothing here hangs on it.

Part by part, between the same rows of before and after, the front came out so:

| Part | from, to | before | after | measured | predicted |
|---|---|---|---|---|---|
| A | start to the turn of s2T | 17.83 | 16.12 | -1.71 | -0.8 |
| | turn to group 0's folds | 11.04 | 11.40 | +0.36 | 0 |
| B | the folds of group 0 | 2.20 | 0.80 | -1.40 | -1.45 |
| C | to a of group 1 | 4.84 | 5.16 | +0.32 | 0 |
| D | to the first pz | 10.57 | 8.62 | -1.95 | -0.2 |
| E | to the end of the u rows | 10.07 | 7.80 | -2.27 | -3.2 |
| F | to up(1) | 8.08 | 10.00 | +1.92 | +2.1 |
| | sum | 64.63 | 59.90 | -4.73 | -3.55 |

- A was sized at half: the bound of -1.5 was passed. In this profile the clock did not do it, since the turns of the exponentials ran as slowly as before (1.12 and 1.11 us after 1.11 and 1.06). Group 0's start 1.70 earlier (9.09 after 10.79) and group 1's 1.27 (10.64 after 11.91), so group 1's scores did not come "a full length later"; that leaves 0.44 for s2T of group 0, issued alone. Where the full clock came sooner, as in e1's profile, the turn of s2T stands 2.82 earlier (15.01). g3 bears out the direction.
- The 0.36 behind A had no term: 0.30 of it is one small row of VectorE, d, which takes 1.16 at 22.66 where it took 0.86.
- B was right, row for row. gl was out of its way, as said.
- D went as its rival "full clock inside D" had it (-1.5): px run at 0.12 from 38.85 in the changed kernel, 5.7 us behind the start of the stream at 33.17, and group 1's waves behind them too. The step "A+2.8" for gl beside the folds was right to 0.05: the fold starts 2.85 behind the transpose. Its cause was another one in part: it stood 1.22 us idle for GpSimd's constants of f, which the program has behind gl.
- E was right in its mechanism and too large by 0.9. The rows of u are back at 0.69 and 0.68, from 1.51 and 1.57. What was overlooked stands ahead of pe, which starts 1.95 behind the first pz (42.10 to 44.05) where it was 1.09 (46.48 to 47.57). ScalarE stands 0.44 for the join on VectorE and then makes wr_h ahead of the first copy of a spectrum; VectorE, busy with the last splits and that join until 43.75, waits 0.30 more for the copy. The row of pe before, and ScalarE's rows after:

```profile
47.57 0.69 DVE L631 TENSOR_TENSOR pe<-px,spec 128x512 f32<-128x512 f32 x1 [0.38 <-ACT spec L609]
```

```profile
43.12 0.62 ACT L99 CAST wr_h<-w1f 128x512 fp32r<-128x512 f32 x1 [0.44 <-DVE w1f L174]
43.65 0.65 ACT L592 COPY spec<-pz 128x258 f32<-128x258 f32 x2
```

- In E the Trainium skill (SBUF — State Buffer, "Who interferes with whom") was quoted for pe and qe losing nothing beside wr_l, since one of their inputs lies in PSUM. The trace agrees: pe takes 0.69 at 44.05, beside wr_l (43.82, 1.29 long), and 0.68 at 47.04, where GpSimd stands still.
- F was right: two joins of 1.78 and 1.75 beside two wr_l, and the hold at the scores, 2.46 us. up(1) starts at 59.90, 0.6 earlier than the range that was named for it.
- Whether the joint folds of batches 1 to 7 are worth the 0.15 that was put for them cannot be read: from up(1) to the last product e1 takes 919.1 and the kernel before 919.4, but the other kernels with steps of 227 ns take 918.6 to 919.7.

The Trainium skill (TensorE: Matmul & The Clock Gate, "Back-to-back issue gap") gives an isolated product at full clock N/2.4 + 2.5 ns, by estimate 215.8 for 512 columns, and about 131 ns for one of a sustained stream, with no term for where the operands lie. The trace differs from both: 226.7 where the operands agree modulo 256, and up to 233.6 where they do not.
